# Decay attention and softplus FFN: lambda spread by a matmul, the opening in a new order, the last bank copied in halves

## The chip, the core and the metric

The kernel runs on one core of one Trainium2 chip. The metric is device time in microseconds (us), the median of several runs. The engines named below are TensorE (PE in the profile; PEld is its weight load), VectorE (DVE), ScalarE (ACT), GpSimd (POOL) and SyncE (SP). SP and ACT also issue the transfers (DMA) between HBM and SBUF; matmuls write to banks of PSUM.

## What is computed

Inputs are `q`, `k`, `v` of shape 4 x 8 x 768 x 64 (batch B, heads H, sequence S, head size D), one decay `lam` for each of the eight heads, and two weights, 512 x 2048 and 2048 x 512. Attention is linear with a decay, in blocks of 64; its output, 3072 tokens of 512, goes through a feed-forward layer with softplus:

```python
Dmask = np.where(rel >= 0, lam[:, None, None] ** rel[None, :, :], 0.0)
for b in range(nb):
    intra = np.einsum('bhic,bhjc->bhij', qb, kb) * Dmask[None]
    intra = np.einsum('bhij,bhjd->bhid', intra, vb)
    inter = np.einsum('bhid,bhde->bhie', qb * lam_pow[None], kv_state)
    out[:, :, sl] = intra + inter
    kv_state = lam_block[None, :, None, None] * kv_state + np.einsum('bhsd,bhse->bhde', kb_dec, vb)
h = x @ w_in
g = np.maximum(h, 0.0) + np.log1p(np.exp(-np.abs(h)))
return (g @ w_out).astype(np.float32)
```

## The kernel before

**Tiling.** The sequence is cut into six chunks of 128 positions; a chunk of all batches is 512 tokens. The eight heads are four pairs, so there are 24 units `g` (chunk x pair), each a tile `att` of 128 x 2 x 2 x 512: q and k with the head size on the partitions ("qk", 512 KB), k and v with the position on them ("kt" and "v", 256 KB each). A unit is loaded whole (1 MB), in halves (`load_half`) or in parts (`load_part`). Chunk 0 has no earlier state and is done as one block of 128.

**Feed-forward.** Products of float32 accuracy are made of three float32r matmuls: the operand is split into a rounded high part and the remainder. `mlp1(s)` makes one 128-row slice of h for one chunk (`s` counts chunk x 16 + slice): four steps `p`, one for each pair, of three matmuls of 128 x 512, in the order high by high, low weight by high x, high weight by low x. `mlp2` multiplies a finished slice into the four output banks of the chunk, 12 matmuls. Between them ScalarE makes the softplus (`act`) and its high part (`ghi`), VectorE the low part (`glo`).

**Weights.** They come as 64-bit words and are turned into float32 pairs on the chip, once. Weight `k` (32 of them, 512 KB each, called raw k) takes seven steps: on ScalarE `scale`, `round`, `hi`; on VectorE `shift`, `sign`, `add`, `lo`. `hi` needs `add`, `lo` needs `hi`. The first six weights are done singly, 512 columns an operation, the others in pairs. Weights 0 to 3 are the first four slices of w_in; then w_out and w_in alternate, so that `mlp 4` needs `lo 5`, `mlp 5` and `mlp 6` need `lo 7` and `lo 9`, and `mlp2 n` needs `lo` of 4 + 2n.

**Attention of chunk 0.** For pair p: `S p` the scores (two banks), `m p t` the mask of head t of the pair (VectorE), `O p` the output, `xh p` and `xl p` its high and low parts (ScalarE, VectorE), the x that `mlp` reads; `kda p` or `kd p` the decay of k (ScalarE or VectorE), `Q p` the sums for the state, `sc p` their copy (ScalarE). For the units 4 to 7 of chunk 1 the steps are `kd1`, `qd`, `sc1`, `m1`, `up`, `out1`, `xh1`, `xl1`.

**Tables.** From lambda the kernel makes, by a running product along the free axis (`powers`, a scan of VectorE): `mask0` (1024 wide, powers below the diagonal of 128), `lp` (512 wide), and from them `mask`, `rp1`, `rp2`, `lam_c`. `lam_b`, lambda on all partitions, comes from a broadcast DMA (line 77). Until the tables stand, nothing of chunk 0 can be masked. `mask0` and its steps lie in the tile `spare`, the starting values in `begin`.

**Order.** Nothing is scheduled automatically: each engine, and each DMA queue, works strictly in the order in which the program issues to it, and waits for what its next instruction needs. The list in lines 586 to 618 is that order for the opening, one name with its numbers for each step; a step may issue to several engines, and `load`, `unit`, `v`, `kt` issue a DMA on SP's queue at that place. `load n` issues all weights below n that have not been issued, `unit n` all units below n. Ahead of the list the loads of line 143 are issued, and `keep_warm(n)` (`warm n` in the list) issues n matmuls on a tile of zeros whose result nobody reads; 13 of them stand at the start. After the list a regular loop (line 637) does the remaining slices, chunk by chunk.

**End.** `mlp2` copies each of the four output banks of a chunk into SBUF when its last matmul is issued, banks 0 and 2 on ScalarE, 1 and 3 on VectorE, and issues its store (lines 484 to 488).

**Buffers.** Tiles of 8 KB a partition (units, raw weights, converted weights, x, `spare`, `begin`, `warm`) share 22 places; PSUM has four banks "o", two "h" and one double bank "t". A new tile waits until the last user of the one that had its place is done.

Of the kernel before, what the change touches and what calls it, by code (L numbers as in the profile page):

```python
# [37 lines left out]
def decay_attention_softplus_ffn(  # L38
# [38 lines left out]
    nc.sync.dma_start(out=lam_b, in_=lam.rearrange("(o h) -> o h", o=1).broadcast_to([128, H]))

# [56 lines left out]

    for queue, s in ((nc.sync, 0), (nc.scalar, 1)):
        queue.dma_start(out=unit(0)[half(s), 0], in_=att[0, 0, half(s), 0])
# [60 lines left out]
    nc.vector.tensor_mul(out=rp1, in0=mask[:, :, T - 1], in1=lam_b)

# [268 lines left out]
    def mlp2(ss):  # L468
        c = ss[0] // NF
        ends = ss[-1] % NF == NF - 1  # L470
        if ss[0] % NF == 0:
            o_tiles[c] = [obank(f"o{c}_{b}") for b in range(B)]
        if ends:
            ob = [t4([128, 2, 512], F32, f"ob{c}_{i}")[:, j] for i in range(2) for j in range(2)]
        for b in range(B):
            for s in ss:
                f = s % NF
                g, w = g_tiles[s], w_of(f, 1)
                for n, (i, j) in enumerate(((0, 0), (0, 1), (1, 0))):
                    nc.tensor.matmul(  # L480
                        o_tiles[c][b], lhsT=g[:, i, b * 128 : (b + 1) * 128], rhs=w[:, j],
                        start=f == 0 and n == 0, stop=f == NF - 1 and n == 2,
                    )
            if ends:
                copy = nc.vector.tensor_copy if b % 2 else nc.scalar.copy
                copy(out=ob[b], in_=o_tiles[c][b])
                queue = nc.scalar if c == NCH - 1 and b % 2 == 0 else nc.sync
                queue.dma_start(out=out[b * S + c * C : b * S + (c + 1) * C, :], in_=ob[b])

# [96 lines left out]
    for line in """  # L586
        S 0, m 0 1, scale 0, shift 0, sign 0, round 0, m 0 0, add 0, warm 3, S 1, scale 1, warm 1, O 0, m 1
        0, hi 0, round 1, xh 0, shift 1, lo 0, sign 1, xl 0, kt 0, m 1 1, kt 1, v 3, round 2, S 2, scale 2,
        load 4, add 1, m 2 0, mlp 0 0, hi 1, load 5, m 2 1, lo 1, O 1, S 3, xh 1, shift 2, load 6, load 7,
        xl 1, kda 0, m 3 1, mlp 1 0, kda 1, m 3 0, sign 2, add 2, scale 3, mlp 1 1, load 8, O 2, xh 2, shift  # L590
        3, xl 2, round 3, hi 2, load 9, O 3, sign 3, lo 2, unit 5, xh 3, kt 2, scale 4, load 10, Q 0, Q 1,
        add 3, scale 5, shift 4, xl 3, hi 3, mlp 1 2, round 5, shift 5, mlp 0 1, sign 4, mlp 2 0, round 4,
        scale 6 7, kt 3, mlp 0 2, mlp 2 1, mlp 0 3, act 0, sc 0, lo 3, ghi 0, unit 6, sign 5, add 4, shift 6
        7, load 11, mlp 1 3, mlp 3 0, add 5, hi 4, hi 5, sign 6 7, mlp 3 1, round 6 7, glo 0, mlp 3 2, lo 5,
        act 1, add 6 7, kd1 4, kd 2, mlp 2 2, ghi 1, mlp 3 3, hi 6 7, glo 1, mlp 2 3, load 12, act 2, mlp 4,
        lo 4, Q 2, kd 3, scale 8 9, ghi 2, lo 6 7, shift 8 9, glo 2, sign 8 9, sc 1, sc1 4, Q 3, up 4, load
        13, sc 2, act 3, mlp 5, sc 3, round 8 9, load 14, scale 10 11, add 8 9, ghi 3, shift 10 11, glo 3,
        mlp2 0, load 15, hi 8 9, load 16, round 10 11, lo 8 9, sign 10 11, m1 4, act 4, mlp2 1, round 12 13,
        load 17, ghi 4, add 10 11, scale 12 13, glo 4, shift 12 13, hi 10 11, kd1 5, lo 10 11, act 5, sign
        12 13, ghi 5, add 12 13, scale 14 15, qd 4, load 18, hi 12 13, mlp 6, glo 5, shift 14 15, mlp2 2,  # L600
        mlp2 3, out1 4, load 19, lo 12 13, load 20, act 6, round 14 15, sign 14 15, load 21, ghi 6, load 22,
        sc1 5, m1 5, add 14 15, load 23, mlp2 4, round 16 17, xh1 4, scale 18 19, scale 16 17, up 5, hi 14
        15, shift 18 19, lo 14 15, mlp 7, load 24, shift 16 17, mlp 8, load 25, unit 7, glo 6, scale 20 21,
        sign 16 17, load 26, act 7, mlp2 5, round 18 19, kd1 6, load 27, add 16 17, hi 16 17, ghi 7, mlp 9,
        qd 5, sign 18 19, lo 16 17, round 20 21, glo 7, add 18 19, unit 8, scale 24 25, load 28, load 29,
        act 8, mlp2 6, xl1 4, ghi 8, glo 8, hi 18 19, out1 5, shift 20 21, act 9, lo 18 19, sc1 6, ghi 9,
        round 22 23, kd1 7, scale 22 23, sign 20 21, mlp2 7, m1 6, add 20 21, mlp 10, shift 22 23, up 6,
        load 30, hi 20 21, shift 24 25, glo 9, scale 28 29, mlp 11, act 10, lo 20 21, ghi 10, mlp2 8, round
        24 25, unit 9, qd 6, glo 10, sign 22 23, act 11, ghi 11, xh1 5, add 22 23, hi 22 23, xl1 5, load 31,
        glo 11, mlp 12, lo 22 23, sign 24 25, add 24 25, act 12, out1 6, sc1 7, m1 7, scale 26 27, shift 26  # L610
        27, ghi 12, round 28 29, hi 24 25, glo 12, sign 26 27, lo 24 25, mlp2 9, xh1 6, shift 28 29, mlp 13,
        load 32, round 26 27, act 13, add 26 27, scale 30 31, sign 28 29, hi 26 27, add 28 29, lo 26 27, xl1
        6, mlp2 10, mlp 14, hi 28 29, ghi 13, glo 13, round 30 31, mlp2 11, shift 30 31, act 14, qd 7, ghi
        14, glo 14, up 7, mlp 15, lo 28 29, act 15, sign 30 31, out1 7, ghi 15, add 30 31, mlp2 12, mlp2 13,
        xh1 7, unit 10, xl1 7, hi 30 31, mlp 16, lo 30 31, glo 15
    """.replace("\n", " ").split(","):
# [89 lines left out]
```

## Time and profile before

| | us |
|---|---|
| median of 3 runs | 592.95 |
| lowest, highest | 592.57, 592.98 |
| the profiled execution's own time | 593.09 |
| its span, first to last instruction | 591.3 |

The page gives busy time of engines and groups of instructions, where "L463" is line 463 of the kernel and "out<-in" the tiles written and read. The timeline lists instructions with start and length in us from the span's start; equal neighbours are merged (x13), and in brackets stands how long the engine had been idle and what ended the wait. The chain of waits goes back from the last instruction, at each step to what released it. Lengths of two neighbours overlap a little, so the distance from start to start is the price of an instruction in a full queue. The costliest groups are the two of the feed-forward, lines 463 and 480, 1152 matmuls each:

```profile
L463 PE MATMUL h<-x,w 128*128 128x512 f32 x1152 | 276.3, 390 | 0.6 <-ACT x L527 0.5
L480 PE MATMUL o<-w,g 128*128 128x512 f32 x1152 | 276.2, 390 | 0.0
raw<-in_wts SPq DMA_DIRECT2D x32, 512.0 KB, 9.3
att<-in_att SPq DMA_DIRECT2D x9, 512.0 KB, 8.8
att<-in_att SPq DMA_DIRECT2D x9, 256.0 KB, 7.5
lam_b<-in_lam SPq DMA_DIRECT2D x1, 4.0 KB, 2.8
```

The last four lines are loads, with the time from issue to landing; in the opening many are in flight at once.

### The profile page before, as it was taken

The numbers are of one execution on the slowest core, as the hardware profiler recorded it, in microseconds if no ns is written. First come the engines' busy times: TensorE is split into PE (matmuls) and PEld (weight loads), VectorE is DVE, ScalarE is ACT, GpSimd is POOL, SyncE is SP. The second block draws the span as 40 slices with busy tenths as digits, with TensorE's granted clock in tenths as the row PEclk, the third lists the DMA queues.
The fourth block names the chain that finished last, engine by engine and source line by source line (L and its number), as shares of the span: only waits on it lengthen the run. The fifth ranks groups of instructions, "written<-read, shape, count | busy, mean of one in ns | idle before, by whom it ended". The sixth has DMA issues, their size and how long they took to land.

```text
span 591.3 us, 10251 instructions
## 1 busy us (share of the span) xinstructions
PE 585.0 (99%) x4465; PEld 484.4 (82%) x4465; DVE 252.0 (43%) x402; ACT 232.1 (39%) x388; POOL 1.5 (0%) x9
## 2 busy tenths in 40 slices
PE   8999999999999999999999999999999999999997
PEld 6778888888888888888888888888888888888885
DVE  8999999658411119621106741012842111201111
ACT  4899868462231363222246132225222122312211
POOL 1000000000000000000000000000000000000000
PEclk9999999999999999999999999999999999999999
DMA  8999230520300211030041030031100000100001
GB/s 284 414 417 418 106 140 6 213 74 2 144 1 1 90 53 73 2 143 0 1 144 72 1 144 1 1 114 47 56 1 2 0 1 0 72 0 1 0 1 71
DMA packets 13309, 48.89 MB, mean 83 GB/s; under 512 B 1617, under 2 KB 1617, under 8 KB 11089
## 3 DMA queue, kind: packets, MB, share of 16 engines
q1 hardware_dynamic: 12896, 47.46, 20.9%
q10 hardware_dynamic: 368, 0.79, 0.4%
q8 instruction: 35, 0.57, 0.4%
q14 instruction: 10, 0.07, 0.0%
HBM read 41.95 MB, written 6.29 MB: 82 GB/s over the span
## 4 chain that ended last, share of the span: by engine, by line
PE 94%; DMA 3%; DVE 1%; SPq 1%; issue 0%; ACT 0%
PE o L480 44%; PE h L463 43%; PE z L333 3%; PE x L302 2%; DMA raw<-in_wts 1%; DMA att<-in_att 1%; DVE c L228 1%; PE w L302 1%; PE y L306 1%; PE z L344 0%; PE x L321 0%; PE z L348 0%; DVE w L241 0%; DVE c L224 0%; DVE c L234 0%
## 5 line engine op out<-in xcount | busy, mean ns | idle before, releaser
L463 PE MATMUL h<-x,w 128*128 128x512 f32 x1152 | 276.3, 390 | 0.6 <-ACT x L527 0.5
L480 PE MATMUL o<-w,g 128*128 128x512 f32 x1152 | 276.2, 390 | 0.0
L463 PEld LDWEIGHTS h<-x,w 128*128 128x128 f32 x1152 | 215.4, 188 | 46.9 <-DVE x L531 0.8
L480 PEld LDWEIGHTS o<-w,g 128*128 128x128 f32 x1152 | 215.6, 188 | 45.2
L452 DVE TENSOR_TENSOR g<-l,g 128x512 fp32r<-128x512 f32 x96 | 66.3, 691 | 309.3 <-ACT g L448 309.3
L444 ACT ACTIVATE l<-h 128x512 f32<-128x512 f32 x96 | 57.4, 598 | 303.8 <-PE h L463 280.5
L448 ACT CAST g<-l 128x512 fp32r<-128x512 f32 x96 | 59.6, 620 | 2.8
L279 ACT ACTIVATE att<-att,rp 64x256 f32<-64x256 f32 x60 | 27.0, 498 | 0.2
L290 DVE TENSOR_TENSOR att<-att,lp 64x512 f32<-64x512 f32 (+1 forms) x42 | 24.6, 585 | 1.1
L355 DVE TENSOR_TENSOR att<-x,mask 64x512 f32<-64x512 f32 (+1 forms) x34 | 19.1, 563 | 6.6 <-PE y L306 4.8
L216 ACT ACTIVATE c<-raw 128x1024 f32<-128x1024 f32 (+1 forms) x19 | 19.0, 1014 | 3.6 <-DMA raw<-in_wts 3.5
L241 DVE TENSOR_TENSOR w<-c,w 128x1024 fp32r<-128x1024 f32 (+1 forms) x19 | 20.0, 1053 | 0.4 <-ACT w L237 0.4
L234 DVE CUSTOM_DVE_ANT_0 c<-raw,c 128x2048 uint16<-128x2048 uint16 (+1 forms) x19 | 20.0, 1053 | 0.3
L228 DVE SCALAR_TENSOR_TENSOR c<-raw,c 128x1024 uint32<-128x1024 uint32 (+1 forms) x19 | 20.0, 1052 | 0.0
L220 ACT ACTIVATE raw<-raw 128x1024 uint32<-128x1024 uint32 (+1 forms) x19 | 19.0, 1009 | 1.2 <-DMA raw<-in_wts 1.2
L237 ACT CAST w<-c 128x1024 fp32r<-128x1024 f32 (+1 forms) x19 | 17.4, 919 | 3.7 <-DVE c L234 3.7
L333 PE MATMUL z<-att 128*64 128x64 f32 x544 | 17.0, 223 | 0.0
L333 PEld LDWEIGHTS z<-att 128*64 128x64 f32 x544 | 16.3, 138 | 0.6 <-issue 0.4
L376 ACT COPY att<-st 64x512 f32<-64x512 f32 (+1 forms) x21 | 11.0, 536 | 12.2 <-PE y L306 11.3
L302 PEld LDWEIGHTS x<-att 64*64 64x64 f32 x416 | 12.9, 135 | 2.8 <-issue 2.8
L422 ACT CAST x<-z 128x512 fp32r<-128x512 f32 x17 | 9.2, 593 | 12.7 <-PE z L333 8.4
L302 PE MATMUL x<-att 64*64 64x64 f32 x416 | 14.1, 220 | 0.0
(69 smaller groups left out, 216.9 us busy)
## 6 DMA issues: line engine op xcount, KB each, us to landing
att<-in_att SPq DMA_DIRECT2D x17, 1024.0 KB, 5.5
raw<-in_wts SPq DMA_DIRECT2D x32, 512.0 KB, 9.3
out_dram<-ob SPq DMA_DIRECT2D x22, 256.0 KB, 2.2
att<-in_att SPq DMA_DIRECT2D x9, 512.0 KB, 8.8
att<-in_att SPq DMA_DIRECT2D x9, 256.0 KB, 7.5
out_dram<-ob ACTq DMA_DIRECT2D x2, 256.0 KB, 2.0
att<-in_att ACTq DMA_DIRECT2D x1, 256.0 KB, 4.9
lam_b<-in_lam SPq DMA_DIRECT2D x1, 4.0 KB, 2.8
```

What stands on the lines that cost most here:

```text
L228: nc.vector.scalar_tensor_tensor(out=c, in0=raw_at(ks, 1), scalar=0x80000000, in1=c, op0=ALU.bitwise_and, op1=ALU.bitwise_or)
L234: nc.vector.tensor_add(out=c, in0=c, in1=raw_at(ks, 0))
L241: nc.vector.tensor_sub(out=w[:, 1], in0=conv.pop(ks[0]).bitcast(F32), in1=w[:, 0])
L279: nc.scalar.activation(k, k, AF.Copy, scale=rp1[r, h : h + 1])
L290: nc.vector.tensor_mul(out=q, in0=q, in1=w[r, bs])
L302: nc.tensor.matmul(x[to, cols], lhsT=region(g, s)[r, b, t], rhs=region(g, 1 - s)[r, b, t], start=True, stop=True)
L333: nc.tensor.matmul(w[half(t), cols], lhsT=region(g, 2 + s)[:, b, t], rhs=region(g, 1 - s)[:, b, t], start=True, stop=True,)
L444: nc.scalar.activation(l_tiles[s], h_tiles.pop(s), AF.Softplus)
L448: nc.scalar.copy(out=g_tiles[s][:, 0, :], in_=l_tiles[s])
L452: nc.vector.tensor_sub(out=g[:, 1, :], in0=l_tiles.pop(s), in1=g[:, 0, :])
L463: nc.tensor.matmul(h_tiles[s], lhsT=w[:, i, cs], rhs=x[:, j, :], start=p == 0 and n == 0, stop=p == NP - 1 and n == 2,)
L480: nc.tensor.matmul(o_tiles[c][b], lhsT=g[:, i, b * 128 : (b + 1) * 128], rhs=w[:, j], start=f == 0 and n == 0, stop=f == NF - 1 and n == 2,)
```

## The change

Four edits that come together. (a) Lambda is loaded as one row on ACT's queue, and a matmul with a row of ones spreads it over the partitions into a PSUM bank, after 4 warm matmuls and ahead of 5 more; the copies that start the tables read that bank, and `lam_b` is copied from it. (b) Of the tables only `mask0` and `rp2` are made ahead of the list; the rest becomes three steps of the list: `tabl` (`lp`, `lam_c`), `taba` (`mask`), `tabr` (`rp1`). (c) The first unit's q and k come as one load on SP instead of two halves on SP and ACT; the loads of line 143 and the whole list are in a new order. The decay of pair 3 moves from VectorE (`kd 3`) to ScalarE (`kda 3`), and fewer warm matmuls are issued. (d) At the very end the last bank is copied in two halves of 256 columns, one by each engine, and stored by two transfers, on SP's and ACT's queues.

```diff
     lam_b = cp.tile([128, H], F32, name="lam_b")
-    nc.sync.dma_start(out=lam_b, in_=lam.rearrange("(o h) -> o h", o=1).broadcast_to([128, H]))
+    lam_row = cp.tile([1, H], F32, name="lam_row")
+    nc.scalar.dma_start(out=lam_row, in_=lam.rearrange("(o h) -> o h", o=1))
+    nc.scalar.preload_act_table_set("softplus")
...
-    for queue, s in ((nc.sync, 0), (nc.scalar, 1)):
-        queue.dma_start(out=unit(0)[half(s), 0], in_=att[0, 0, half(s), 0])
-    nc.scalar.preload_act_table_set("softplus")
+    load_half(0, 0)
...
-    for line in "w 1, qk 1, w 2, v 0, qk 2, v 1, w 3, qk 3, v 2".split(","):
+    for line in "w 1, qk 1, w 2, kt 0, v 0, qk 2, v 1, qk 3, w 3".split(","):
...
-    keep_warm(13)
+    ones = cp.tile([1, 128], F32, name="ones")
+    nc.gpsimd.memset(ones, 1.0)
+    lam_ps = bank("lam_ps")
+    keep_warm(4)
+    nc.tensor.matmul(lam_ps[:, :H], lhsT=ones, rhs=lam_row, start=True, stop=True)
+    keep_warm(5)
...
     def lam_over(n):
-        return lam_b.rearrange("q (h o) -> q h o", o=1).broadcast_to([128, H, n])
+        return lam_ps[:, :H].rearrange("q (h o) -> q h o", o=1).broadcast_to([128, H, n])
...
     powers(mask0, step0, begin0)
-    powers(lp, step1, begin1)
+    nc.vector.tensor_copy(out=lam_b, in_=lam_ps[:, :H])
     nc.vector.tensor_mul(out=rp2, in0=mask0[:, :, C - 1], in1=lam_b)
-    nc.vector.tensor_mul(out=lam_c, in0=lp[:, :, T - 1], in1=lam_b)
-    for s in range(2):
-        nc.scalar.copy(out=mask[half(s)], in_=mask0[half(s), :, s * T : (s + 1) * T])
-    nc.vector.tensor_mul(out=rp1, in0=mask[:, :, T - 1], in1=lam_b)
+
+    def table_powers():
+        powers(lp, step1, begin1)
+        nc.vector.tensor_mul(out=lam_c, in0=lp[:, :, T - 1], in1=lam_b)
+
+    def table_mask():
+        for s in range(2):
+            nc.scalar.copy(out=mask[half(s)], in_=mask0[half(s), :, s * T : (s + 1) * T])
+
+    def table_decay():
+        nc.vector.tensor_mul(out=rp1, in0=mask[:, :, T - 1], in1=lam_b)
...
+            if not ends:
+                continue
+            parts = [(slice(0, 512), b % 2 == 0)]
+            if c == NCH - 1 and b == B - 1:
+                parts = [(slice(0, 256), False), (slice(256, 512), True)]
+            for cols, act in parts:
+                copy = nc.scalar.copy if act else nc.vector.tensor_copy
+                copy(out=ob[b][:, cols], in_=o_tiles[c][b][:, cols])
+                queue = nc.scalar if c == NCH - 1 and act else nc.sync
+                queue.dma_start(out=out[b * S + c * C : b * S + (c + 1) * C, cols], in_=ob[b][:, cols])
...
+                round 0, S 0, scale 0, tabl, m 0 1, shift 0, m 0 0, sign 0, warm 2, S 1, scale 1, round 1, m 1 1,
+        shift 1, warm 1, O 0, v 2, m 1 0, kda 0, sign 1, add 0, S 2, taba, hi 0, xh 0, add 1, hi 1, O 1,
+        scale 2, m 2 1, m 2 0, S 3, v 3, load 4, round 2, lo 0, xl 0, kt 3, m 3 0, m 3 1, xh 1, Q 0, O 2, lo
+        1, load 5, sc 0, load 6, xl 1, xh 2, O 3, load 7, round 3, mlp 1 0, scale 3, load 8, tabr, kt 1,
+        shift 2, xl 2, kt 2, sign 2, mlp 1 1, kda 3, shift 3, xh 3, unit 5, scale 4, load 9, scale 5, add 2,
+        mlp 0 0, load 10, mlp 0 1, hi 2, mlp 1 2, round 4, sign 3, xl 3, add 3, mlp 0 2, shift 5, hi 3, load
+        11, mlp 0 3, act 0, scale 6 7, ghi 0, lo 2, mlp 1 3, lo 3, shift 4, kda 1, sign 5, shift 6 7, load
+        12, load 13, sign 4, unit 6, round 5, round 6 7, kd 2, add 4, hi 4, mlp 2 0, add 5, kd1 4, hi 5, mlp
+        3 0, mlp 2 1, glo 0, sign 6 7, lo 5, mlp 2 2, mlp 3 1, act 1, mlp 2 3, mlp 3 2, add 6 7, ghi 1,
+        scale 8 9, mlp 3 3, Q 1, glo 1, Q 2, shift 8 9, load 14, sc1 4, load 15, hi 6 7, lo 6 7, act 2, sc
+        2, Q 3, ghi 2, sc 1, load 16, lo 4, glo 2, sign 8 9, sc 3, up 4, act 3, mlp 4, mlp 5, load 17, round
+        8 9, load 18, ghi 3, scale 10 11, add 8 9, glo 3, hi 8 9, act 4, scale 12 13, shift 10 11, load 19,
+        unit 7, lo 8 9, round 10 11, mlp2 0, round 12 13, load 20, sign 10 11, mlp2 1, load 21, ghi 4, shift
+        12 13, add 10 11, sign 12 13, hi 10 11, kd1 5, glo 4, act 5, mlp 6, unit 8, scale 14 15, load 22,
+        mlp2 2, load 23, lo 10 11, load 24, ghi 5, m1 4, add 12 13, qd 4, glo 5, mlp2 3, hi 12 13, act 6,
+        scale 16 17, shift 14 15, lo 12 13, out1 4, sc1 5, load 25, round 14 15, sign 14 15, m1 5, up 5, add
...
```

The old list, line by line, is in the kernel above; the rest of the new one has the same steps up to `mlp 16` in an order of its own.

More of the change, by code (lines that the diff above doesn't have):

```diff
@@ L483, in mlp2 @@
                     )
[L484 to L488, printed above, removed]
+            if not ends:
[8 more added lines that the diff above has]
+                queue.dma_start(out=out[b * S + c * C : b * S + (c + 1) * C, cols], in_=ob[b][:, cols])
     def w_group(j):
@@ L576, in decay_attention_softplus_ffn @@
     step = {
-        "S": scores0, "m": mask0_scores, "O": out0, "xh": x0_high, "xl": x0_low, "kd": k0_decay, "kda": k0_decay_act,
+        "tabl": table_powers, "taba": table_mask, "tabr": table_decay, "S": scores0, "m": mask0_scores, "O": out0, "xh": x0_high, "xl": x0_low, "kd": k0_decay, "kda": k0_decay_act,
         "Q": sums0, "sc": states0, "kd1": k_decay, "qd": q_decay, "sc1": scores1,
@@ L586, in decay_attention_softplus_ffn @@
     for line in """
[L587 to L615, printed above, removed]
+                round 0, S 0, scale 0, tabl, m 0 1, shift 0, m 0 0, sign 0, warm 2, S 1, scale 1, round 1, m 1 1,
@@ new lines, in decay_attention_softplus_ffn @@
+        14 15, ghi 6, glo 6, load 26, mlp2 4, round 16 17, xh1 4, scale 20 21, shift 16 17, mlp 7, hi 14 15,
+        act 7, lo 14 15, mlp 8, qd 5, sign 16 17, shift 20 21, ghi 7, load 27, scale 18 19, round 22 23, mlp
+        9, mlp2 5, glo 7, xl1 4, out1 5, round 18 19, shift 18 19, act 8, kd1 6, unit 9, ghi 8, add 16 17,
+        glo 8, hi 16 17, sign 18 19, act 9, round 20 21, ghi 9, lo 16 17, add 18 19, sc1 6, scale 22 23,
+        load 28, m1 6, mlp2 6, hi 18 19, shift 22 23, mlp 10, sign 20 21, glo 9, kd1 7, lo 18 19, sign 22
@@ new lines, in decay_attention_softplus_ffn @@
+        23, load 29, act 10, add 20 21, load 30, scale 24 25, add 22 23, load 31, hi 20 21, lo 20 21, ghi
+        10, glo 10, mlp2 7, hi 22 23, qd 6, mlp 11, act 11, mlp2 8, shift 24 25, round 26 27, round 24 25,
+        lo 22 23, sign 24 25, xh1 5, mlp 12, scale 26 27, up 6, ghi 11, scale 28 29, glo 11, xl1 5, act 12,
+        add 24 25, mlp2 9, round 28 29, out1 6, shift 28 29, hi 24 25, load 32, sc1 7, shift 26 27, lo 24
+        25, m1 7, xh1 6, mlp2 10, mlp 13, up 7, scale 30 31, sign 26 27, ghi 12, add 26 27, mlp 14, shift 30
@@ L616, in decay_attention_softplus_ffn @@
+        31, hi 26 27, glo 12, lo 26 27, mlp2 11, sign 28 29, act 13, ghi 13, add 28 29, glo 13, xl1 6, qd 7,
+        hi 28 29, act 14, lo 28 29, ghi 14, glo 14, round 30 31, mlp 15, sign 30 31, out1 7, unit 10, mlp2
+        12, xh1 7, act 15, xl1 7, add 30 31, mlp2 13, ghi 15, hi 30 31, glo 15, mlp 16, lo 30 31
     """.replace("\n", " ").split(","):
```

## The prediction

> **What bounds the kernel now.** First the page: span and busy time of each engine.
>
> ```profile
> span 591.3 us, 10251 instructions
> PE 585.0 (99%) x4465; PEld 484.4 (82%) x4465; DVE 252.0 (43%) x402; ACT 232.1 (39%) x388; POOL 1.5 (0%) x9
> ```
>
> Then the view of windows, which splits busy time by stage (its clock column reads 1.00 throughout and tells nothing here):
>
> ```profile
> core 0: us, PE busy (x) PEld busy (x) DVE busy (x) ACT busy (x) POOL busy (x), PEclk, DMA share, GB/s
> 16.00:22.00 6.00, 5.50 (x87) 4.70 (x85) 4.94 (x10) 3.43 (x8) 0.00 (x0) 1.00 1.04 415
> 22.00:37.00 15.00, 14.93 (x148) 11.59 (x149) 15.00 (x24) 14.76 (x27) 0.00 (x0) 1.00 1.03 417
> 37.00:112.00 75.00, 75.00 (x712) 61.90 (x712) 72.61 (x91) 59.72 (x82) 0.00 (x0) 1.00 0.51 202
> ```
>
> Last the chain of waits in order of time (start, length, what):
>
> ```profile
> 4.10 8.22 DMA att<-in_att
> 12.34 8.38 DMA raw<-in_wts
> 31.70 2.79 PE h L463 x11
> 36.81 2.95 PE h L463 x12
> 39.76 5.44 PE o L480 x24
> 45.20 2.72 PE h L463 x12
> ```
>
> TensorE is busy 99% of the span, but the chain is its own without a break only from 31.70; before that it runs through two long transfers and VectorE. From 37 to 112 TensorE has no idle time, with VectorE at 72.61 of 75 us beside it. TensorE's work is fixed, so a new order can win in two places: in the opening, where TensorE waits, and behind the last matmul. My yardstick for the opening is the start of `mlp2 0`, the row at 39.76: in both orders the same work lies ahead of it (scores, outputs and sums of chunk 0, `sc1 4`, `mlp 0` to `mlp 5`). If nothing stalls later, the kernel's time moves as this row does.
>
> **VectorE's path in the new opening.** Its prices, from the timeline (start, length) and one group of the view by lines:
>
> ```profile
> 3.58 0.69 DVE L190 COPY spare<-lam_b 128x1016 f32<-128x1016 f32 x1 [1.44 <-DMA lam_b<-in_lam]
> 4.38 2.29 DVE L185 TENSOR_TENSOR_SCAN spare<-spare,begin 128x1024 f32<-128x1024 f32 x1
> 6.59 1.20 DVE L185 TENSOR_TENSOR_SCAN lp<-begin 128x512 f32<-128x512 f32 x1
> 7.98 0.17 DVE L198 TENSOR_TENSOR rp<-mask,lam_b 128x8 f32<-128x8 f32 x1
> 8.34 0.69 DVE L512 TENSOR_TENSOR att<-x,spare 128x512 f32<-128x512 f32 x1 [0.19 <-PE x L506]
> 11.80 0.42 DVE L224 TENSOR_SCALAR c<-c 128x512 uint32<-128x512 uint32 x1
> 12.14 0.69 DVE L241 TENSOR_TENSOR w<-c,w 128x512 fp32r<-128x512 f32 x1
> 12.74 0.69 DVE L228 SCALAR_TENSOR_TENSOR c<-raw,c 128x512 uint32<-128x512 uint32 x1
> 21.45 0.43 DVE L224 TENSOR_SCALAR c<-c 128x512 uint32<-128x512 uint32 x1 [0.98 <-ACT c L216]
> 38.70 1.79 DVE L366 SCALAR_TENSOR_TENSOR st<-st,lam_c,w 64x256 f32<-64x256 f32 x4
> 587.51 0.69 DVE L486 COPY ob<-o 128x512 f32<-128x512 f32 x1 [2.03 <-PE o L480]
> L241 DVE TENSOR_TENSOR w<-c,w 128x1024 fp32r<-128x1024 f32 x13 | 15.9, 1221 | 0.4 <-ACT w L237 0.4
> ```
>
> and TensorE's, for the sums that follow:
>
> ```profile
> 1.45 5.75 PE L155 MATMUL warm_ps<-warm 128*128 128x512 f32 x13 [1.45 <-DVE warm L150]
> 8.22 0.96 PE L155 MATMUL warm_ps<-warm 128*128 128x512 f32 x3
> 18.55 1.97 PE L521 MATMUL z<-att 128*64 128x128 f32 x32
> 20.35 1.10 PE L550 MATMUL y<-att 128*64 128x64 f32 x32
> 34.42 0.69 PE L550 MATMUL y<-att 128*64 128x64 f32 x16
> ```
>
> Lambda. Before, the copy of lambda into the scan's steps starts at 3.58, when the broadcast lands. Now a row must land: no row shows so small a load; it takes at least nothing and at most about what the broadcast takes, so it is there by 3.6. Its matmul stands behind four warm matmuls, from 1.45 at 0.44 each (5.75/13), and issues near 3.2; with the row landed by then, the copy starts near 3.65. Behind this wait stand five warm matmuls and `S 0`, which nobody needs earlier. The copy now reads PSUM. From SBUF 1016 elements take 0.69 (3.58); from PSUM 512 take the same (587.51). By proportion 1016 from PSUM take up to 1.4, at least 0.69; I take 1.2, proportion less a fixed part, as the PSUM row is the nearer. ScalarE's copy of the other steps lies beside the scan. Then 0.11 to the scan, 2.21 to the next operation (4.38 to 6.59), two 8-element operations 0.25, and `tabl` (scan 1.12, product 0.17) ahead of the first mask: `m 0 1` starts at 3.65 + 1.31 + 2.21 + 0.25 + 1.29 = 8.7 against 8.34. **The tables lose 0.4.** `taba` on ScalarE and `tabr` (0.15 of VectorE) are first needed by `kd1 4` and `m1 4`, beyond 28.
>
> In-order sum. Start to start, a 512-element operation costs 0.60 (12.14 to 12.74), a `shift` 0.34 (11.80 to 12.14). From `m 0 1` up to `m 3 1` the new list has 13 of the first and two of the second, 8.5, and 0.1 for an operation that waits for its neighbour: `m 3 1` starts at 17.3 and ends at 18.0. `O 3` needs it and starts at 18.1. The other things `O 3` needs, `v 3` (one piece behind `v 2`, near 17) and, for `O 2` ahead of it, the bank that `xl 0` frees near 16.7, are earlier.
>
> **TensorE from there.** `O 3` costs 0.90 (18.55 to 20.35 for two); `mlp 0` to `mlp 3`, 48 matmuls of 2.72/12 = 0.227, 10.88; `Q 2`, `sc1 4`, `Q 3` 2.39 (34.42 to 36.81) and `Q 1` 0.55; `mlp 4` and `mlp 5` 5.44; three changes between small and large matmuls 0.24 each (2.95 against 2.72). Sum 20.9: `mlp2 0` would start at 39.0 against 39.76, **gain 0.8**, if TensorE doesn't stall between. The tight places are `lo 2` and `lo 3`. From `m 0 1` to `lo 2` stand 22 operations of 0.60, five shifts and `tabr`, 15.05, and 0.2 for dependent neighbours: `lo 2` starts at 24.0 and ends at 24.7. `mlp 2 0` reaches its second matmul, the first that reads it, at 18.1 + 0.90 + 0.24 + 24 x 0.227 + 0.23 = 24.9. `lo 3` follows if `hi 3` is done, and that hangs on the transfers.
>
> **The transfers.**
>
> ```profile
> 0.73 0.38 SPq L77 DMA_DIRECT2D lam_b<-in_lam  x1
> 1.16 0.54 SPq L137 DMA_DIRECT2D att<-in_att  x1
> 3.30:7.00 3.70, 3.70 (x10) 2.64 (x8) 3.31 (x3) 0.91 (x2) 0.00 (x0) 1.00 0.94 245
> 7.00:16.00 9.00, 8.50 (x91) 6.26 (x92) 8.78 (x18) 6.32 (x12) 0.00 (x0) 1.00 1.03 414
> 20.74 0.68 ACT L216 ACTIVATE c<-raw 128x512 f32<-128x512 f32 x1 [2.27 <-DMA raw<-in_wts]
> 24.48 0.63 ACT L237 CAST w<-c 128x512 fp32r<-128x512 f32 x1
> 24.99 1.26 ACT L220 ACTIVATE raw<-raw 128x512 uint32<-128x512 uint32 x2
> ```
>
> At 414 GB/s a 512 KB piece takes 1.27. Up to raw 5 both orders issue 6656 KB, so its place in the stream is the same: before, raw 3 landed at 20.72 (12.34 + 8.38) and raw 5 two pieces later, 23.2. raw 3 was late: from 12.32 to 20.72 eight pieces, 2816 KB, should take 7.0 and took 8.4. I keep these 1.4 us, since nothing in the change removes them. What may help is an earlier start of the stream: SP's queue no longer begins with the broadcast, its first piece moves from 1.16 to 0.73 and is whole instead of two halves on two queues. Bounds: nothing, or 3.7 us x (414 - 245) = 625 KB, 1.5 us, if the stretch up to 7 ran at full rate. I take 0.8, half way, as no row decides. Then on ScalarE `scale 5` starts at 22.4, `hi 2` 0.57 later, `round 4` 0.51 after that (24.48 to 24.99), `hi 3` 0.57 on, done in 0.63 at 24.7. `lo 3` runs from 24.7 to 25.4, and `mlp 3 0` wants it at 25.6. With no shift it ends at 26.2, and TensorE loses 0.6. raw 3, with one 256 KB piece fewer ahead of it (0.6), lands at 19.3; `scale 3` and `xh 3` behind it are then done 0.3 and 0.6 before `shift 3` and `xl 3`.
>
> The Trainium skill ("Trainium Kernel Development and Optimization", Key Constraints) says that the SP, ACT and POOL queues share the same 16 DMA engines and that issuing from several saves only the sequencer's issue time. By it the shift would be 1.16 - 0.73 = 0.4 and the opening's gain 0.6; the 245 GB/s suggest more, and no run here tells.
>
> **After the yardstick.** Pair operations cost 1.22 less 0.08, 1.14; `up 4` 1.83. From `lo 3` to `lo 8 9` the new list has 15 of 0.60, one of 0.34, five of 1.14 and `up 4`, 16.9: it ends at 43.0, and `mlp 6` wants it at 39.0 + 5.44 = 44.4. Continued so, `lo 10 11` ends at 48.9 for `mlp2 3` at 49.9 and `lo 12 13` at 53.7 for `mlp2 4` at 54.9; later pairs have about as much. ScalarE, blocked at `act 10` to `act 12` until their `mlp` ends, delays `lo 20 21` by 0.6, inside a margin of 1.6. raw 28 and raw 30 wait for buffers that `add 16 17` and `add 18 19` free near 65 and 70 and are needed near 86 and 95. So no stall.
>
> **The tail.** The price of a copy of 256 columns on ScalarE, the issues of the last outputs, and (of that tile alone) their time to landing:
>
> ```profile
> L558 ACT COPY st<-y 64x256 f32<-64x256 f32 x5 | 1.9, 370 | 0.0
> 585.51 3.05 SPq L488 DMA_DIRECT2D out_dram<-ob  x2
> DMA to landing us min/median/max: 2.0/2.0/2.0
> ```
>
> The last copy, 0.69 (587.51), becomes two of 256 columns on two engines: 0.37 on ScalarE, and about 0.42 on VectorE (0.69 less 256 of the 512 elements at 0.27). That saves 0.27. The two transfers start together and move the same bytes; I give them the same 2.0, and 0.06 for one more completion. **Gain 0.2** (bounds 0 and 0.4).
>
> **Sum.** 0.8 + 0.2 = 1.0. The profiled execution took 593.09 (span 591.3, 1.8 around it) and would take 592.1; from the median of 592.95 it is 592.0.
>
> **Rivals.** (1) The stream doesn't start earlier: the opening gains 0.2, the kernel takes 592.6. For it: raw 5 keeps its place in the stream. Against: SP's first issue comes 0.43 earlier. (2) The PSUM copy costs no more than the SBUF copy and the stream gains over 1: `m 0 1` at 8.2, all else 0.5 earlier, 591.5, with the best tail 591.3. For it: 245 GB/s. Against: 512 elements from PSUM in 0.69. (3) Slower: **the clock**. The first 13 warm matmuls come 0.44 apart, the three at 8.22 take 0.96 together, so the rate rose near 7. Of the 13 nine are left, ending near 5.5 with a wait among them; then TensorE stands until `S 0`. If full rate comes late, the small products take twice their time. Until 10.3 this costs 0.1, as VectorE leads. If it lasts to 19, the chain `O 0`, `S 2`, `O 1`, `S 3` (0.9 to 1.2 each, doubled from 11 on) puts `O 3` at 20.8, 2.7 later, and the kernel at 594.7. It decides from about 14 us on. Against: those four follow closely and keep TensorE busy.
>
> The Trainium skill ("TensorE: Matmul & The Clock Gate", Part 1) has the clock released after a window of some 3.4 us of sustained work, with windows that run freely; 3.9 us of warm matmuls with a gap could fall astride two. The 5.75 us without a gap, before, fit it but cannot show that.
>
> **Chances.** Forecast 0.45, (1) 0.2, (2) 0.25, (3) 0.1. A measurement here tells 0.2%, 1.2 us: faster, below 591.76, is (2) and a quarter of the forecast, 0.36; slower, above 594.1, is (3), 0.1; the rest, 0.54, is within. Range 591.1 to 593.2: (2) with 0.2 to spare, (1), and a clock late by one window.
>
> **What would show it.** Right: L190's copy from PSUM near 1.2, `m 0 1` near 8.7, `O 3` near 18.1, TensorE unbroken from there, `mlp2 0` near 39.0; raw 5 landing near 22.4; the last copy near 0.4. Wrong: a stall at `mlp 2 0` or `mlp 3 0`, matmuls 0.43 apart after 8, or an `mlp` or `mlp2` that waits for a `lo` between 40 and 110.

## The result and the profile after

| | median us | lowest to highest | profiled execution | its span |
|---|---|---|---|---|
| before | 592.97 | 592.57 to 593.01 | 593.09 | 591.3 |
| changed | 597.08 | 596.55 to 598.41 | 597.53 | 595.7 |

The changed kernel is slower, by less than one per cent but clear of the noise: ratio 1.0074, 95% interval 1.0063 to 1.0085, or 4.1 us. That lies outside the range of the prediction, on the other side of no change. The page of the changed kernel, span and busy time:

```profile
span 595.7 us, 10245 instructions
PE 587.1 (99%) x4462; PEld 486.1 (82%) x4462; DVE 251.5 (42%) x402; ACT 232.9 (39%) x391; POOL 1.7 (0%) x10
```

TensorE still stands at 99%, so the page alone hides the loss: 4.4 us of span are less than one per cent. The view of TensorE's waits (engine, tile, line, whom it waited for: total, times, longest) shows one that the kernel before doesn't have:

```profile
PE y L567 <- ACT st L575: 2.8, 1, 2.8
```

L567 is `sums0`, L575 is `states0`. TensorE's timeline around it (start, length, operation; in brackets the idle time before it and who ended it):

```profile
19.44 11.98 PE L475 MATMUL h<-x,w 128*128 128x512 f32 x48
31.35 1.15 PE L567 MATMUL y<-att 128*64 128x64 f32 x32
...
36.38 0.69 PE L567 MATMUL y<-att 128*64 128x64 f32 x16 [2.79 <-ACT st L575]
37.00 7.35 PE L475 MATMUL h<-x,w 128*128 128x512 f32 x24
44.19 5.60 PE L492 MATMUL o<-w,g 128*128 128x512 f32 x24
```

The 32 matmuls at 31.35 are `Q 1` and `Q 2`, then come `sc1 4` (left out) and, after 2.79 us of nothing, `Q 3`. Behind it `mlp 4` and `mlp 5` take 7.35 us for 24 matmuls, which take 5.44 at full rate. The last row is `mlp2 0`, the yardstick. In the kernel before the row of `Q 3` has no bracket, so no wait, and `mlp2 0` begins at 39.60:

```profile
36.13 0.69 PE L550 MATMUL y<-att 128*64 128x64 f32 x16
...
39.60 5.60 PE L480 MATMUL o<-w,g 128*128 128x512 f32 x24
```

So 4.6 us are lost ahead of the yardstick, and 0.2 are won back behind it (the spans differ by 4.4). ScalarE's timeline of the changed kernel, up to the copy that releases `Q 3`:

```profile
33.13 1.16 ACT L228 ACTIVATE c<-raw 128x1024 f32<-128x1024 f32 x1
34.18 1.04 ACT L249 CAST w<-c 128x1024 fp32r<-128x1024 f32 x1
35.11 0.61 ACT L456 ACTIVATE l<-h 128x512 f32<-128x512 f32 x1
35.60 0.73 ACT L575 COPY st<-y 64x256 f32<-64x256 f32 x2
```

These are `scale 8 9`, `hi 6 7`, `act 2` and `sc 2`, back to back. In the new list `sc 2` stands ahead of `Q 3`. `sums0` puts the sums of pairs 2 and 3 into two halves of one PSUM tile (`y[p // 2]`); `sc 2` reads the first half, `Q 3` writes the second. The built program has `Q 3` wait for ScalarE:

```
L567 MATMUL y2_398<-att3_82 64x64 [waits Activation_49]
```

So TensorE, free from 33.6 on, stands until ScalarE has worked through its queue. In the kernel before, `Q 3` stood ahead of `sc 2` and nothing had to be waited for. What the Trainium skill says of this ("PSUM — Partial Sum Buffer", PSUM bank collisions raise a hardware error): two engines may not touch one bank in the same 32 partitions at once, reads included, whatever the columns, so software orders them. By it the wait can't be dropped, only the order or the bank changed; no run here shows a collision.

The clock, from the view of windows (its bounds set to 3.41 us; PEclk is the granted clock):

```profile
core 0: us, PE busy (x) PEld busy (x) DVE busy (x) ACT busy (x) POOL busy (x), PEclk, DMA share, GB/s
33.85:37.26 3.41, 0.88 (x17) 0.81 (x18) 3.33 (x6) 3.36 (x8) 0.00 (x0) 1.00 1.03 408
37.26:40.67 3.41, 3.41 (x9) 2.64 (x9) 3.31 (x6) 3.35 (x7) 0.00 (x0) 0.50 1.02 406
40.67:44.08 3.41, 3.41 (x16) 2.78 (x16) 3.41 (x4) 3.08 (x4) 0.00 (x0) 1.00 1.03 411
```

TensorE was busy for 0.88 us of the first window and ran the whole next one at 0.50. Half of 3.41 is 1.7 us lost; by the rows above, `mlp 4` and `mlp 5` lose 7.35 less 5.74, 1.6, against the run of experiment 1. Theory: 2.8 of wait and 1.7 of clock are the whole loss, and one swap in the list undoes both.

### The profile page after: what moved, and what is told of

The parts are those of the page before. It is cut to its first block, busy times and chain, and to the rows that moved or that the text cites. A ratio compares the mean times of both kernels' runs of the same rounds, so it can differ in the third digit from the quotient of the medians.

```text
span 595.7 us, 10245 instructions
## 1 busy us (share of the span) xinstructions
PE 587.1 (99%) x4462; PEld 486.1 (82%) x4462; DVE 251.5 (42%) x402; ACT 232.9 (39%) x391; POOL 1.7 (0%) x10
## 4 chain that ended last, share of the span: by engine, by line
PE 93%; DMA 3%; ACT 2%; SPq 1%; issue 0%; DVE 0%
PE o L492 44%; PE h L475 42%; PE z L345 3%; PE x L314 2%; DMA raw<-in_wts 2%; DMA att<-in_att 2%; PE w L314 1%; PE y L318 0%; ACT c L228 0%; ACT w L249 0%; ACT raw L232 0%; PE z L356 0%; SPq L89 0%; PE x L333 0%; ACT l L456 0%
```

## The experiments

Each kernel is compared with the kernel before on the same chip. Interval means the 95% interval of the ratio to it.

### 1. Q 3 ahead of sc 2

```diff
-    act 2, sc 2, Q 3, ghi 2,
+    act 2, Q 3, sc 2, ghi 2,
```

> The changed kernel with one swap in its list: Q 3 is written ahead of sc 2 instead of behind it; everything else as in the changed kernel. Theory A (the two share one PSUM tile, so Q 3 behind sc 2 has to wait for ScalarE's read; the wait of 2.79 us and the half clock behind it are the whole loss): no wait ahead of Q 3, no matmuls 0.43 us apart in mlp 4 and mlp 5, mlp2 0 starts near 39.8 instead of 44.35 (44.35 less 2.8 less 1.75), the kernel takes 592.3 to 592.8. Theory B (the clock gate halves the rate there whatever TensorE waited for, or another order of the chunk's end is late): the wait goes or is replaced by another one near 36, mlp2 0 stays beyond 41, the kernel stays above 594.

Measured: 592.66 us, ratio 0.9995 (0.9986 to 1.0003), against 592.93 before. TensorE's timeline:

```profile
19.43 11.42 PE L475 MATMUL h<-x,w 128*128 128x512 f32 x48
...
32.95 0.69 PE L567 MATMUL y<-att 128*64 128x64 f32 x16
33.57 5.74 PE L475 MATMUL h<-x,w 128*128 128x512 f32 x24
39.14 5.60 PE L492 MATMUL o<-w,g 128*128 128x512 f32 x24
```

`Q 3` has no bracket, so no wait; the 24 matmuls take 5.74 with the time of the first; the yardstick is at 39.14. One swap brings back 4.4 us in the medians and 5.0 in the profiled executions (44.19 to 39.14): 2.8 of wait, 1.6 of clock, and 0.56 in `mlp 0` to `mlp 3` (11.98 against 11.42), where raw 5 landed at 23.5 in the one and at 22.95 in the other. Theory A holds. The rest of the change is worth 0.27 us in the medians, and the interval allows for anything from 0.8 us faster to 0.2 slower.

### 2. The fault put into the kernel before

```diff
-    sc 1, sc1 4, Q 3, up 4, load 13, sc 2,
+    sc 1, sc1 4, up 4, load 13, sc 2, Q 3,
```

> The kernel before with the suspected fault put in: Q 3 written behind sc 2 (and behind up 4), all else as before. Theory A (shared tile): Q 3, which started at 34.42, now waits for ScalarE's sc 2, some 1 to 3 us, and if the idle time is long enough the clock halves behind it: 594 to 597.5. If the wait is there but the clock stays full, the time rises by the wait alone. Theory B (the loss comes from the other parts of the change): no change, 592.7 to 593.2.

Measured: 594.55 us, ratio 1.0025 (1.0016 to 1.0035), 1.6 slower. Its row of `Q 3`, then the window that holds the wait and the one after it:

```profile
37.64 0.69 PE L550 MATMUL y<-att 128*64 128x64 f32 x16 [1.46 <-ACT st L558]
```

```profile
36.55:39.96 3.41, 2.32 (x23) 1.97 (x24) 3.34 (x7) 3.19 (x7) 0.00 (x0) 1.00 1.03 420
39.96:43.37 3.41, 3.41 (x16) 2.81 (x15) 3.38 (x6) 3.37 (x5) 0.00 (x0) 1.00 1.03 416
```

The same order costs here too, without anything else of the change. `Q 3` begins 1.5 later than the 36.13 of the kernel before (the 34.42 of the expectation is the row of `Q 2`). The wait is shorter, since ScalarE comes to `sc 2` sooner after TensorE is ready, and the clock stays full: the time rises by 1.6, about the wait alone.

### 3. The wait kept, TensorE busy in it

```diff
+    "again": lambda g: mm_scores(g, *xy[g]),
-    act 2, sc 2, Q 3, ghi 2,
+    act 2, sc 2, again 4, again 4, Q 3, ghi 2,
```

> The changed kernel with Q 3 still behind sc 2, but sc1 4's 64 small matmuls issued twice more in between (they write the same values again), so that TensorE works through most of the wait. Theory A1 (the wait costs 2.8 us and the idle time itself brings the half clock, 1.75 us more): Q 3 starts when it did, the matmuls of mlp 4 and mlp 5 come 0.23 apart, mlp2 0 near 42.6, the kernel takes 595.2 to 595.6. Theory A2 (the half clock comes of something else, such as the many small matmuls): the clock is half from 37 on all the same, 597 as in the changed kernel.

Measured: 595.78 us, ratio 1.0045 (1.0033 to 1.0057). Timeline of TensorE, then the window that ran at half rate in the changed kernel:

```profile
36.01 0.69 PE L567 MATMUL y<-att 128*64 128x64 f32 x16 [0.27 <-ACT st L575]
```

```profile
37.26:40.67 3.41, 3.41 (x17) 2.79 (x16) 3.31 (x7) 3.36 (x6) 0.00 (x0) 1.00 1.02 396
```

`Q 3` comes nearly as late as it did (36.01 against 36.38), but the clock is 1.00 and 17 matmuls begin where 9 did. All executions agree: their mean granted clock is 0.999 or 1.000 in the five of this kernel and 0.993 to 0.997 in the six of the changed one, where 3.41 us at half rate take 0.003 off. The median lies 0.2 above the expectation's bound, the profiled execution (595.48) within it. This parts the loss, if roughly, as the changed kernel was measured on its own: from the run with `Q 3` first to this one 3.1 us (592.66 to 595.78) for the wait, from here to the changed kernel 1.3 in the medians and 2.05 in the profiled executions (595.48 to 597.53), of which 0.37 had been lost ahead of `Q 3` (36.38 against 36.01) and 1.6 to 1.7 is the clock. So A1: the idle time brings the half rate.

### 4. The halved tail alone

The kernel before with part (d) of the change:

```diff
+            parts = [(slice(0, 512), b % 2 == 0)]
+            if c == NCH - 1 and b == B - 1:
+                parts = [(slice(0, 256), False), (slice(256, 512), True)]
```

> The kernel before with the last bank's copy in two halves alone. As forecast: one copy of 0.69 becomes two side by side, 0.2 less, 592.75. As the changed kernel's trace reads (ScalarE's half starts only when VectorE's has ended, 0.42 and 0.37 one after the other, but two stores of half the size on two queues that land 0.2 sooner): between 0 and 0.2 less, 592.75 to 592.97.

Measured: 592.66 us, ratio 0.9996 (0.9988 to 1.0005): 0.27 less, a little more than either reading expected, and the interval holds 1. The tail's rows of VectorE and ScalarE, and the yardstick of this run:

```profile
587.04 0.43 DVE L491 COPY ob<-o 128x256 f32<-128x256 f32 x1 [2.03 <-PE o L480]
...
587.50 0.37 ACT L491 COPY ob<-o 128x256 f32<-128x256 f32 x1 [1.23 <-DVE ob L491]
```

```profile
39.21 5.60 PE L480 MATMUL o<-w,g 128*128 128x512 f32 x24
```

The halves don't run side by side. ScalarE had been free for 1.23 us and starts when VectorE ends: both read one PSUM tile, and the program orders them. They end 0.83 after the first began, later than the one copy of 0.69. Yet from that start to the end of the span it is 3.56 (590.6 less 587.04) against 3.79 before (591.3 less 587.51), since the last store, half as large, takes 2.7 from its issue to the end (587.91 to 590.6) instead of 3.1 (588.23 to 591.3).

The yardstick is as telling. This kernel's opening is that of the kernel before, and `mlp2 0` begins at 39.21, not at 39.60. Two executions of one opening thus differ by 0.4 at this row: the one from which the prediction took its baseline was slower than its kernel's median (593.09 against 592.95), this one faster (592.39 against 592.66). Against 39.21, the 39.14 of experiment 1 is a gain of 0.07. The medians say the same: this kernel and experiment 1 have the same tail, and both take 592.66, so the new opening gains nothing that can be told from the noise.

### 5 and 8. Where the big tiles begin in SBUF

Why did the stream of transfers bring nothing? The windows view gives 404 GB/s from 22 to 34 for the changed kernel (first row) against 416 before (second row):

```profile
22.00:34.00 12.00, 11.37 (x135) 8.67 (x133) 11.59 (x20) 11.80 (x21) 0.00 (x0) 1.00 1.03 404
22.00:34.00 12.00, 11.93 (x50) 9.15 (x51) 12.00 (x20) 11.88 (x21) 0.00 (x0) 1.00 1.03 416
```

Lambda's new tile takes 32 bytes of a partition and with the row of ones moves all tiles behind it by 544 bytes: `att0` from 5888, which is 23 times 256, to 6432. Two edits:

```diff
-    lam_row = cp.tile([1, H], F32, name="lam_row")
+    lam_row = cp.tile([1, 2 * H], F32, name="lam_row")[:, :H]
```

> The changed kernel with Q 3 ahead of sc 2, and the tile of lambda's row 16 numbers wide instead of 8 (64 bytes in a partition instead of 32; the load still fills 8). The new tile of 32 bytes had moved every tile behind it in SBUF by 32 bytes, so that the transfers' targets no longer begin at a multiple of 64 bytes. Theory S (that start is why the stream runs at 405 GB/s from 22 on and 376 from 7 to 16, against 415 and 414 before): both go back to about 414, raw 5 lands at 21.9 to 22.4 instead of 22.95, the wait of 0.39 of VectorE for hi 3 goes; the kernel gains 0 to 0.5, as VectorE's own row then binds: 592.2 to 592.7. Theory N (the rate comes of the whole first piece, of the second queue or of the new order of pieces): 405 and 376 stay.

```diff
     lam_b = cp.tile([128, H], F32, name="lam_b")
+    shift32 = cp.tile([1, H], F32, name="shift32")
+    nc.gpsimd.memset(shift32, 0.0)
```

> The kernel before with one more tile of 32 bytes (8 numbers, cleared by GpSimd) behind lam_b, so that all tiles behind it begin 32 bytes further; nothing else. Theory S: the stream falls from 414 to 375 to 405 GB/s, raw 3 lands 0.5 to 1 later than 20.72, the kernel takes 593.2 to 594. Theory N: the stream stays at 414 and the kernel at 592.93.

Measured: the padded row 592.46 us, ratio 0.9992 (0.9983 to 1.0001), with 405 GB/s, as good as unchanged by the padding; the shifted kernel before 593.57, ratio 1.0012 (1.0002 to 1.0021). The windows rows, first of the padded row, then of the shifted kernel before:

```profile
22.00:34.00 12.00, 11.97 (x152) 9.54 (x151) 11.67 (x19) 11.97 (x22) 0.00 (x0) 1.00 1.03 405
```

```profile
22.00:34.00 12.00, 11.46 (x48) 8.73 (x49) 11.96 (x20) 11.89 (x22) 0.00 (x0) 1.00 1.03 404
```

The shift of 32 bytes alone slows the old stream by 3%, and the kernel by 0.6 us, an interval that just leaves out 1. A start at a multiple of 64 doesn't mend it.

### 9. Lambda's row in 256 bytes

```diff
-    lam_row = cp.tile([1, H], F32, name="lam_row")
+    lam_row = cp.tile([1, 64], F32, name="lam_row")[:, :H]
```

> The changed kernel with Q 3 ahead of sc 2, and lambda's row in a tile of 256 bytes in a partition, so that the tiles behind it begin at a multiple of 256 bytes, as in the kernel before (with 64 bytes the stream stayed at 405 and 366 GB/s, while the shift of 32 bytes alone slowed the kernel before to 404). Theory S256 (the transfers want a start at a multiple of more than 64 bytes): packets of 4096 bytes take 159 ns again, the stream runs at 414 to 418 from 7 on, raw 5 lands near 22.2, VectorE's wait for hi 3 goes, 592.1 to 592.5. Theory T (the dip from 10 to 12.5 comes of something else in the row's kernel, the alignment is only the 2.5% behind it): 415 from 16 on, but still 360 to 380 from 7 to 16, raw 5 at 22.5 or later, 592.3 to 592.7.

Measured: 592.33 us, ratio 0.9989 (0.998 to 0.9998). Windows:

```profile
7.00:16.00 9.00, 8.22 (x93) 6.48 (x93) 8.93 (x18) 5.76 (x11) 0.00 (x0) 1.00 1.01 368
22.00:34.00 12.00, 12.00 (x153) 9.62 (x152) 11.66 (x20) 11.97 (x22) 0.00 (x0) 1.00 1.03 416
```

At a multiple of 256 bytes the rate is 416 again, so the start of the tiles is shown as the cause of the 3%. The slow stretch from 7 to 16 (368 GB/s) is something else, as theory T had it. VectorE's wait for `hi 3` doesn't go, though:

```profile
25.34 0.69 DVE L253 TENSOR_TENSOR w<-c,w 128x512 fp32r<-128x512 f32 x1 [0.34 <-ACT w L249]
```

### 6 and 7. Lambda's broadcast on the other queue

Edit 6, on experiment 1, undoes lambda's edit but for the queue; edit 7 moves `kt 3` and `kda 3` as well:

```diff
-    lam_row = cp.tile([1, H], F32, name="lam_row")
-    nc.scalar.dma_start(out=lam_row, in_=lam.rearrange("(o h) -> o h", o=1))
+    nc.scalar.dma_start(out=lam_b, in_=lam.rearrange("(o h) -> o h", o=1).broadcast_to([128, H]))
...
+    keep_warm(13)
```

```diff
-    lo 0, xl 0, kt 3, m 3 0, m 3 1, xh 1, Q 0, O 2, lo 1, load 5, sc 0,
+    lo 0, xl 0, m 3 0, m 3 1, xh 1, Q 0, O 2, lo 1, load 5, kt 3, sc 0,
...
-    mlp 1 1, kda 3, shift 3, xh 3,
+    mlp 1 1, shift 3, xh 3,
...
-    hi 3, load 11,
+    hi 3, kda 3, load 11,
```

> The changed kernel with Q 3 ahead of sc 2 and the edit of lambda undone: the broadcast load again (now on ScalarE's queue), the copies from SBUF, 13 warm matmuls in one row; the tables in three steps, the new order and the halved tail stay. Without the new tile the big tiles lie as before too. If VectorE's row from lambda to lo 2 and lo 3 is what sets the opening: the first mask at 8.1 to 8.4 instead of 9.21, mlp2 0 0.4 to 0.9 ahead of the run with the padded row, the kernel 591.6 to 592.0. If the transfers bind as well (raw 5 and hi 3): 0 to 0.3 ahead, 592.1 to 592.5.

> As the kernel with lambda's edit undone, and kt 3 (256 KB, not needed before Q 3) loaded behind raw 5 instead of ahead of raw 4, with kda 3 behind hi 3. raw 5 lands 0.62 sooner. If raw 5 through hi 3 binds the opening once VectorE is earlier: mlp2 0 another 0.3 to 0.6 earlier, 591.3 to 591.8. If VectorE alone binds: no change, or 0.1 to 0.5 later where kda 3 stands in ScalarE's way.

Measured: 596.28 us, ratio 1.0052 (1.0039 to 1.0065), and 595.42, ratio 1.0048 (1.0035 to 1.0061). Both miss by 4, for a reason that neither theory had. VectorE's timeline of the first, and its windows:

```profile
7.29 0.69 DVE L189 COPY spare<-lam_b 128x1016 f32<-128x1016 f32 x1 [5.15 <-DMA lam_b<-in_lam]
```

```profile
9.44:12.85 3.41, 0.76 (x6) 0.57 (x8) 3.34 (x7) 2.10 (x6) 0.00 (x0) 0.99 1.04 413
12.85:16.26 3.41, 3.41 (x27) 2.75 (x27) 2.96 (x7) 1.15 (x3) 0.00 (x0) 0.51 1.02 412
```

Beside a 512 KB piece on the other queue, the 4 KB of the broadcast land at 7.3 instead of 3.56. TensorE then stands for want of a mask, and the next window runs at half rate; in the profiled execution of edit 7 two windows do. This is like the prediction's rival (3), half rate and a doubled chain in the opening, but the rate fell again after it had risen, and in a kernel that isn't the changed one. As tests of lambda's edit these two say nothing.

### 10, 11 and 12. Lambda's broadcast first on SP; kt 3 behind raw 5

Edit 10 changes one word of edit 6; 11 is 10 with the moves of 7, and 12 is experiment 9 with them.

```diff
-    nc.scalar.dma_start(out=lam_b, in_=lam.rearrange("(o h) -> o h", o=1).broadcast_to([128, H]))
+    nc.sync.dma_start(out=lam_b, in_=lam.rearrange("(o h) -> o h", o=1).broadcast_to([128, H]))
```

> The changed kernel with Q 3 ahead of sc 2 and the edit of lambda undone as the kernel before has it: the broadcast goes first on SP's queue (on ScalarE's queue beside the first piece it landed at 7.27 instead of 3.56), then the whole first piece; copies from SBUF, 13 warm matmuls in one row. The first mask starts near 8.05 instead of 9.21, O 3 some 1.1 earlier, raw 5 lands at 22.2 to 23.1. If VectorE's row alone set the opening: mlp2 0 1.0 earlier than in the run with Q 3 first (39.3), 591.4 to 591.8. If raw 5 through hi 3 and lo 3 binds as well: mlp2 0 at 38.8 to 39.2, a wait of near 1 us in TensorE at mlp 3 0, 592.0 to 592.5.

> As the run with lambda's broadcast first on SP's queue, and kt 3 loaded behind raw 5, with kda 3 behind hi 3. raw 5 lands 0.62 sooner. If raw 5 binds: mlp2 0 0.3 to 0.6 earlier than in that run, 591.6 to 592.0, ahead of both kernels. If it doesn't: the same as that run, or 0.1 to 0.5 later where kda 3 stands in ScalarE's way.

> As the run with lambda's row in 256 bytes, and kt 3 loaded behind raw 5, with kda 3 behind hi 3. In this order VectorE's row, 1.1 later than with the broadcast first, should bind and not raw 5: 0 to 0.2 earlier than without the move, 592.0 to 592.5. A gain of 0.4 or more would say that raw 5 binds here too.

Measured: 592.37 us, ratio 0.999 (0.9981 to 0.9999); 592.75, 0.9998 (0.9989 to 1.0007); 592.58, 0.9994 (0.9985 to 1.0003). In experiment 10 the first mask runs at 8.30, 0.9 ahead of the kernels with lambda's row, and the kernel is no faster than experiment 9: the second theory's time, not the first's. Its wait of near 1 us in TensorE isn't there, though: the 48 matmuls of `mlp 0` to `mlp 3` take 11.65, only 0.2 more than the 11.42 of experiment 1. Its timelines, VectorE's and ScalarE's:

```profile
8.30 0.69 DVE L522 TENSOR_TENSOR att<-x,spare 128x512 f32<-128x512 f32 x1 [0.27 <-PE x L516]
...
25.14 0.69 DVE L246 TENSOR_TENSOR w<-c,w 128x512 fp32r<-128x512 f32 x1 [0.34 <-ACT w L242]
```

```profile
19.77 0.67 ACT L225 ACTIVATE raw<-raw 128x512 uint32<-128x512 uint32 x1 [0.61 <-DMA raw<-in_wts]
```

That is ScalarE's last wait for a long time: from raw 3's landing at 19.75 (`round 3`) it works without a break, and `hi 3`, which `lo 3` at 25.14 waits for, stands at the end of that row. In experiment 9 the same row begins at 19.96 and `lo 3` at 25.34, each 0.2 later, and `mlp2 0` is 0.2 later too (39.22 against 39.02). So the opening seems to hang on raw 3 and ScalarE's queue behind it, and most of what VectorE gains ahead of it is lost by `lo 3`. This is read from the traces; no run moved raw 3. Moving `kt 3` gains nothing in either kernel (0.38 and 0.25 more in the medians), which fits, as raw 3 lies ahead of it; in experiment 11's profiled execution gaps in TensorE brought another window at half rate as well:

```profile
8.45:11.86 3.41, 1.75 (x18) 1.16 (x17) 2.83 (x7) 2.09 (x5) 0.00 (x0) 1.00 1.03 412
11.86:15.27 3.41, 3.36 (x30) 3.06 (x32) 2.35 (x4) 3.37 (x7) 0.00 (x0) 0.50 1.03 417
```

The best versions, 9 and 10, are 0.1% faster than the kernel before; their intervals just leave out 1.

## Why the prediction was wrong

**The step that failed** is TensorE's sum: "gain 0.8, if TensorE doesn't stall between", with `lo 2` and `lo 3` as the "tight places". `Q 3` stood in that sum as work alone, part of the 2.39 us of `Q 2`, `sc1 4` and `Q 3`, with no wait. That its PSUM tile is read by `sc 2`, now ahead of it in the list and behind `scale 8 9`, `hi 6 7` and `act 2` on ScalarE, was left out. In its place the runs showed a wait of 2.79 us on ScalarE and a window at half rate behind it. In the medians, step by step from kernel to kernel, 0.3 is gained, 3.1 goes to the wait and 1.3 to the clock, together the 4.1 slower.

**The rival with the clock** had the mechanism, gave it a chance of 0.1 and a time of 594.7, and put it at the wrong place. At the start the rate did come late, at no cost that shows; TensorE's rows of the changed kernel:

```profile
8.42 1.22 PE L155 MATMUL warm_ps<-warm 128*128 128x512 f32 x2
9.57 1.54 PE L523 MATMUL x<-att 64*128 64x128 f32 x16
```

Two warm matmuls still take 0.61 each, where three took 0.96 together at 8.22 before, but VectorE, at its tables until 9.21, led anyway. In experiment 1, with the same opening, the two warm matmuls take 0.73 together from 8.09, and `mlp 1 0` begins at 19.43 in the one and 19.44 in the other: the late rate cost nothing. The idle time that mattered was the one that the sum had left out.

**The tables** lost 0.9, not 0.4. Rows of the changed kernel:

```profile
4.08 1.22 DVE L195 COPY spare<-lam_ps 128x1016 f32<-128x1016 f32 x1 [1.81 <-PE lam_ps L161]
...
9.21 0.69 DVE L529 TENSOR_TENSOR att<-x,spare 128x512 f32<-128x512 f32 x1
```

The PSUM copy was sized right (1.2 forecast, 1.22 measured); it began at 4.08 instead of 3.65, since lambda's matmul ended only then. But next to nothing of the price was paid: experiments 9 and 10, with the first mask at 9.21 and at 8.30, take the same time (592.33 and 592.37).

**The sums by start-to-start prices** came out close, in part by luck: in experiment 1 `lo 2` began at 24.17 against 24.0 forecast, though the row had begun 0.5 late, so that the sum behind it was 0.3 too long; `mlp2 0` began at 39.14 against 39.0. The gain of 0.8 did not hold. Its baseline of 39.76 was read from the chain of waits, where the timeline, from which the prices came, has 39.60 for the same row (the chain puts experiment 1's at 39.30, not 39.14): that is 0.16. Another 0.39 is what two executions of the old opening differ by (39.60 against 39.21 in experiment 4), and 0.14 the later start (39.14 instead of 39.0). 0.07 is left.

**The transfers**: no shift of 0.8; raw 5 was there at 23.5 instead of 22.4 (22.95 in experiment 1), as this row of the changed kernel's ScalarE says:

```profile
23.55 0.67 ACT L228 ACTIVATE c<-raw 128x512 f32<-128x512 f32 x1 [0.17 <-DMA raw<-in_wts]
```

The stream did start earlier, and gave it back: 361 GB/s from 7 to 16, and 3% less behind that, by the tiles' start. Rival (1), the stream no earlier and 592.6, has the time that experiment 1 measured (592.66), but not its mechanism, and that is luck: the stream did start earlier, and the opening gained 0.07 and not 0.2.

**The tail** gained 0.27 in the medians, not clear of the noise, and 0.23 in the rows (3.79 less 3.56), against 0.2 forecast. That is luck, since its mechanism was wrong: the copies run one after the other and lose 0.14 (0.83 against 0.69), and the last store, which the forecast left as it was, gains 0.4. **After the yardstick** there is no stall once `Q 3` is in its place: from `mlp2 0` to the end of the span it takes 551.6 us (590.7 less 39.14), experiment 4 with the old list 551.4.

## What to carry to other kernels

When an order by hand changes, walk each PSUM tile, not only each engine: a matmul moved behind a read of its tile waits for the whole queue of the engine that reads. A wait on TensorE is dear beyond its length, since the window after it can run at half rate; where it can't be avoided, filling it with matmuls that write the same values again saved the second part here. And one profiled execution can be 0.4 us off at a row on which a gain of 0.8 is reckoned; a second kernel with the same opening tells.
